# Block attention and MLP on one core: output transposes moved behind the weights' transposes and into their own half of the outputs' bank

## The chip, the cores and the metric

The kernel runs on one core of a Trainium2 chip. The metric is the device time of one execution in microseconds (us). An execution is also profiled: a hardware trace gives start and duration of every instruction on TensorE (PE, with its weight loads as PEld), VectorE (DVE), ScalarE (ACT), GpSimd (POOL) and of the DMA queue that SyncE (SP) issues.

## The reference

Block-sparse attention feeds an MLP. There are 4 batches, 8 heads, 768 positions and 64 values per head; positions come in 24 blocks of 32.

```python
scores = q @ k.T / sqrt(64)
mask = |blk_i - blk_j| <= 1, or blk_i or blk_j is the first or last block,
       or blk_j is one of three sampled blocks of blk_i
attn = softmax(where(mask, scores, -1e9))
x = (attn @ v).transpose(0, 2, 1, 3).reshape(3072, 512)
h = maximum(x @ w_in, 0)                  # w_in 512 x 2048
out = (s * h * h + b) @ w_out             # w_out 2048 x 512
```

Everything is in float32.

## The kernel before

**Slots.** The attention of the first and last query block against all keys is "dense", that of the other 22 query blocks "sparse" (their own three blocks, the two edge blocks, three sampled ones). The work is cut into 52 slots. A sparse slot is one query block of two batches (44 slots, of 22 for each pair of batches), with four units of work; a dense slot is a group of heads of the edge blocks of one batch (8 slots, two units each). Their order is the list `ORD` (line 31): four dense slots, the first pair's sparse slots, four more dense slots woven between the last of these and the first of the second pair's, then the rest.

**A sparse slot.** TensorE makes scores (`scores`, L962) into halves of two PSUM banks. VectorE scales and masks them and takes the row minimum of the negated scores (`maximum`, L980), ScalarE takes the exponential (`exp`, L993). TensorE transposes these weights, eight 128x128 transposes into two banks t (`transposes`, L1023); VectorE evicts the first bank and ScalarE the second (`evacuate`, L1039 and L1041). TensorE multiplies by the values, 64 small matmuls (`av`, L1089; called AV below), into half of the outputs' bank xs; halves alternate from slot to slot. VectorE scales the outputs by one over the row sums into xss (`x_scale`, L1095), TensorE transposes them, two 128x128 transposes (`x_transpose`, L1104; called the pair below), ScalarE copies them to xst (`x_copy`, L1109; four buffers), and SP stores them to DRAM (`spill`, L1116), from where the MLP loads them.

**Dense outputs.** Dense slots evict their weights transposed into dp and the like and wait; 16 sparse slots add 32 matmuls each (`av_dense`, L1079) that sum all eight groups' outputs of two batches in one bank od, a quarter for each slot. When the last of these has run, four dense outputs leave: scale, one transpose within its own quarter of od, copy, two store DMAs (L1120).

**Where the pair stands and where it writes.** Six banks (0 to 5) rotate among scores and t; bank 6 is od and bank 7 is xs. Before the change the pair of slot i-1 stands in slot i between the scores of slot i+2 and the AV of slot i. It writes into the first t bank of slot i, which VectorE has by then evicted; where slot i is dense or missing it takes the next half of xs.

**The order of work.** `Plan` (L109) is a list scheduler that runs when the program is built: each step has an engine, a cost, a priority, dependencies (`deps`, finished first) and places in a queue (`order`, started first), and buffers that it takes (`alloc`) or reads (`use`), with a capacity each (`xst` 4, `xss` 2, `o` 2, `B` 6). TensorE's order in attention is written out by hand (`line`, L1357 to L1365); the other engines take, of what can start first, the step of least priority number. For outputs that is the slot's unit number minus 12, for evictions the unit number minus 8, for exponentials the unit number itself. In the finished program an engine works its queue in order, and semaphores hold each step for the data and buffers that it touches. Decoding of the MLP's weights (L85 to L95) is woven into attention on VectorE, ScalarE and GpSimd. The MLP's first products (L443 to L445) follow attention, its second ones (L485 to L487) wait until all outputs have left the banks they need (`every`, L1373).

Of the kernel before, what the change touches and what calls it, by code (L numbers as in the profile page):

```python
# [212 lines left out]
def kernel(  # L213
# [452 lines left out]
    with ExitStack() as es:  # L666
# [343 lines left out]
        def transposes(n, g):  # L1010
# [4 lines left out]
            if g == 0:  # L1015
                tbank[n] = tp
# [26 lines left out]
        xs_of, xst_of, xss_of, tr_of, tbank = {}, {}, {}, {}, {}  # L1043
# [9 lines left out]
        def goes_on(i):  # L1053
            return i + 1 < len(slots) and slots[i + 1][0] == "s"

        def out_of(i, j):
            if i not in xs_of:
                xs_of[i], tr_of[i] = next_half().rearrange("p (h d) -> p h d", h=4), None
            return xs_of[i][:, j, :]
# [32 lines left out]
        def x_scale(i):  # L1092
            xs = xs_of.pop(i)
            xss = xss_of[i] = xp.tile([P, 4, D], F32, tag="xss", name=f"xss{i}")[:, :xs.shape[1], :]
            nc.vector.tensor_tensor(out=xss, in0=xs, in1=rcs.pop(i).unsqueeze(2).broadcast_to(list(xs.shape)), op=ALU.mult)  # L1095

        def x_transpose(i):
            tr = tr_of[i]
            if tr is None:
                tr = tbank[unit_of[i + 1]][:, :2 * P] if goes_on(i) else next_half()  # L1100
                tr = tr_of[i] = tr.rearrange("p (a q) -> p a q", q=P)
# [4 lines left out]
        def x_copy(i):  # L1106
            tr = tr_of[i]
            xst_of[i] = xp.tile([P, 2, P], F32, tag="xst", name=f"xst{i}", bufs=4)[:, :tr.shape[1], :]
# [73 lines left out]
        spills, tensor, lqs, before, globs = {}, {}, {}, {}, []  # L1182
# [3 lines left out]
        for i, (kind, e, k, r) in enumerate(slots):  # L1186
# [121 lines left out]
            if i and tensor[i - 1][3] and not dense:  # L1308
                tensor[i - 1][3][0].deps.append(evs[0][0])
# [14 lines left out]
            def ends_of(i, u, o_av, dense):  # L1324
                key, rc = (("od", slots[i][1] // 2), ("rd", i)) if dense else (("o", i), ("rc", i))
                to = key if dense else ("B", ("t", unit_of[i + 1], 0)) if goes_on(i) else ("o", ("x", i))
                xc = op("v", 300 if dense else 430, u + T["XA"], lambda i=i: x_scale(i), [o_av, drc[i] if dense else o_rc], alloc=[("xss", i)], use=[key, rc])
                tr = op("p", 270 if dense else 365, u, lambda i=i: x_transpose(i), [xc], cols=256 if dense else 512, use=[("xss", i), to] if dense or goes_on(i) else [("xss", i)], alloc=[] if dense or goes_on(i) else [to])
                ac = op("a", 280 if dense else 390, u + T["XA"], lambda i=i: x_copy(i), [tr], alloc=[("xst", i)], use=[to])
                spills[i] = op("s", 1150 if dense else 600, u + T["SPP"], lambda i=i: spill(i), [ac], use=[("xst", i)], nbytes=66e3 if dense else 131e3)  # L1330
                return tr, ac, xc
# [3 lines left out]
            if k % NBC == 1:  # L1335
# [10 lines left out]
                if not left:  # L1346
                    room = len(slots) - 1 - i
                    for n, m in enumerate(y for y, sl in enumerate(slots) if sl[0] == "d" and sl[1] // 2 == e):
                        late.setdefault(i + 1 + n * min(room, 4) // 4, []).append(ends_of(m, u + 4 + 4 * n, pav, True))
            tensor[i] = s_ops, t_ops, a_ops, trs  # L1350
            before[r] = s_ops, reads
        for i, x in late.items():
            before_it = [tensor[y][3][0] for y in range(i) if tensor[y][3]]
            for n, (tr, _, xc) in enumerate(x):
                xc.deps.append(before_it[-1 if n else -2])
            late[i] = [tr for tr, _, _ in x]
        line = tensor[0][0] + tensor[1][0]  # L1357
# [8 lines left out]
        leave = {id(x) for y in tensor.values() for x in y[3]} | {id(x) for y in late.values() for x in y}  # L1366
# [249 lines left out]
```

## Time and profile before

| | |
|---|---|
| device time, median of 3 runs | 761.25 us (759.11 to 766.74) |
| the profiled execution | 760.56 us |
| its span, first to last instruction | 758.9 us |
| TensorE busy | 732.5 us (97%), 8032 matmuls |
| VectorE, ScalarE, GpSimd busy | 567.8, 472.7, 284.8 us |
| granted TensorE clock, mean | 0.998 |
| share of the chain that ended last: output transposes into t / outputs L1089 / scores L962 / weights' transposes L1023 | 2% / 5% / 5% / 5% |

Attention takes the first 240 us, the MLP the rest. A line such as "PE t L1104" names an engine, the tile that is written and the line of the kernel. In a view of waits, "A <- B" means that engine A was idle until B finished; "issue" means that no semaphore explains the idle time. In a timeline each row is a start, a duration (of a merged run of instructions, first start to last end), engine, line, operation, output<-inputs, and in brackets the idle time of the engine before it.

### The profile page before, as it was taken

The numbers are of one execution on the slowest core, as the hardware profiler recorded it, in microseconds if no ns is written. First come the engines' busy times: TensorE is split into PE (matmuls) and PEld (weight loads), VectorE is DVE, ScalarE is ACT, GpSimd is POOL, SyncE is SP. The second block draws the span as 40 slices with busy tenths as digits, with TensorE's granted clock in tenths as the row PEclk, the third lists the DMA queues.
The fourth block names the chain that finished last, engine by engine and source line by source line (L and its number), as shares of the span: only waits on it lengthen the run. The fifth ranks groups of instructions, "written<-read, shape, count | busy, mean of one in ns | idle before, by whom it ended". The sixth has DMA issues, their size and how long they took to land.

```text
span 758.9 us, 21400 instructions
## 1 busy us (share of the span) xinstructions
PE 732.5 (97%) x8032; PEld 624.0 (82%) x8032; DVE 567.8 (75%) x1436; ACT 472.7 (62%) x1141; POOL 284.8 (38%) x477
## 2 busy tenths in 40 slices
PE   7899999999898999999989999999999999999997
PEld 6576766777677998988878998989989888898896
DVE  3866668988776999987797687797677688666652
ACT  3866668988776887888644443675434566345433
POOL 4977777668641112220022322233222232223221
PEclk9999999999999999999999999999999999999999
DMA  9779778767665346536232230233000022000002
GB/s 266 212 237 282 232 223 240 213 184 217 199 185 155 111 117 217 167 111 161 77 98 83 89 114 28 63 110 86 0 1 1 1 63 84 1 1 0 1 1 83
DMA packets 98743, 89.41 MB, mean 118 GB/s; under 512 B 50352, under 2 KB 79664, under 8 KB 98640
## 3 DMA queue, kind: packets, MB, share of 16 engines
q1 hardware_dynamic: 92544, 71.40, 31.3%
q0 software_dynamic: 6096, 16.65, 7.8%
q8 instruction: 63, 1.03, 0.6%
q14 instruction: 40, 0.33, 0.1%
HBM read 69.15 MB, written 14.68 MB: 110 GB/s over the span
## 4 chain that ended last, share of the span: by engine, by line
PE 84%; DVE 6%; DMA 3%; ACT 3%; issue 2%; SPq 1%; ACTq 0%; DVEq 0%
PE m L622 21%; PE o L486 11%; PE o L487 11%; PE o L485 11%; PE xs L1089 5%; PE s L962 5%; PE t L1023 5%; PE h L443 3%; PE h L445 3%; PE h L444 3%; PE od L1079 2%; PE t L1104 2%; PE t L1021 2%; PE s L941 2%; DVE ptile L980 1%
## 5 line engine op out<-in xcount | busy, mean ns | idle before, releaser
L464 POOL TENSOR_TENSOR hid<-hid,hid 128x384 fp32r<-128x384 f32 x96 | 105.5, 1100 | 297.3 <-ACT hid L640 276.9
L639 ACT ACTIVATE hid<-hid,sb_b,sb_s 128x384 f32<-128x384 f32 x96 | 68.0, 708 | 151.5 <-DVE hid L633 151.5
L993 ACT ACTIVATE ptile<-ptile,nm 128x256 f32<-128x256 f32 (+1 forms) x208 | 107.5, 520 | 45.4 <-DVE nm L980 45.2
L980 DVE CUSTOM_DVE_ANT_1 ptile<-s,mt 128x256 f32<-128x256 f32 x176 | 64.4, 419 | 16.5 <-PE s L962 16.3
L487 PE MATMUL o<-woutr,hid 128*128 128x512 f32 x168 | 66.5, 396 | 0.0
L486 PE MATMUL o<-woutr,hid 128*128 128x512 f32 x168 | 66.3, 395 | 0.0
L485 PE MATMUL o<-woutr,hid 128*128 128x512 f32 x168 | 65.3, 389 | 0.0
L622 PE MATMUL m<-wout,win 128*128 128x384 f32 x264 | 62.2, 339 | 1.0 <-ACT xrest L1509 1.0
L622 PE MATMUL m<-xp,wop 128*128 128x384 f32 x288 | 58.3, 337 | 0.0
L486 PE MATMUL o<-win,hid 128*128 128x512 f32 x144 | 56.8, 395 | 0.0
L633 DVE SCALAR_TENSOR_TENSOR hid<-hid 128x384 f32<-128x384 f32 x96 | 54.3, 565 | 3.3
L622 PE MATMUL m<-xp,win 128*128 128x384 f32 x288 | 55.0, 337 | 1.4 <-DVE xp L606 0.7
L1023 PE MATMUL t<-ident,ptile 128*128 128x128 f32 x352 | 54.5, 297 | 0.5 <-issue 0.5
L622 PEld LDWEIGHTS m<-xp,win 128*128 128x128 f32 x288 | 51.0, 188 | 4.3 <-DVE xp L606 1.2
L640 ACT CAST hid<-hid 128x384 fp32r<-128x384 f32 x96 | 49.4, 514 | 7.8 <-PE o L487 0.4
L622 PEld LDWEIGHTS m<-xp,wop 128*128 128x128 f32 x288 | 51.5, 188 | 2.1
L1023 PEld LDWEIGHTS t<-ident,ptile 128*128 128x128 f32 x352 | 45.7, 208 | 6.7 <-issue 1.1
L907 POOL COPY kk<-kt 128x256 f32 x132 | 50.4, 417 | 0.0
L622 PEld LDWEIGHTS m<-wout,win 128*128 128x128 f32 x264 | 47.5, 188 | 3.3 <-ACT xrest L1509 1.4
L487 PE MATMUL o<-win,hid 128*128 128x512 f32 x126 | 49.8, 395 | 0.0
L485 PE MATMUL o<-win,hid 128*128 128x512 f32 x126 | 49.2, 391 | 0.2
L632 DVE TENSOR_TENSOR hid<-m,xrest 128x384 f32<-128x384 f32 x48 | 26.5, 551 | 30.5 <-issue 25.7
(195 smaller groups left out, 1884.3 us busy)
## 6 DMA issues: line engine op xcount, KB each, us to landing
vB<-in_v_dram SPq DMA_DIRECT2D x76, 128.0 KB, 3.9
raw_o<-in_w_out_dram SPq DMA_DIRECT2D x14, 512.0 KB, 3.6
raw_i<-in_w_in_dram SPq DMA_DIRECT2D x12, 512.0 KB, 3.8
vA<-in_v_dram POOLq DMA_DIRECT2D x46, 128.0 KB, 3.7
xd<-xst SPq DMA_DIRECT2D x44, 128.0 KB, 3.8
vA<-in_v_dram SPq DMA_DIRECT2D x42, 128.0 KB, 4.1
out_dram<-ob SPq DMA_DIRECT2D x20, 256.0 KB, 2.0
sum<-xd SPq DMA_DIRECT2D x12, 384.0 KB, 4.6
```

The lines of the kernel that those rows point to most:

```text
L464: (eng or nc.vector).tensor_tensor(out=htile(5 + i % 3), in0=t, in1=gh.bitcast(F32), op=ALU.subtract)
L485: nc.tensor.matmul(acc, gh[:, tsl], wout(f, 0), start=first, stop=False)
L486: nc.tensor.matmul(acc, gh[:, tsl], wout(f, 1), start=False, stop=False)
L487: nc.tensor.matmul(acc, gl[:, tsl], wout(f, 0), start=False, stop=last)
L622: nc.tensor.matmul(to, w_, x_, start=(c == 0 and k == 0), stop=(c == 1 and k == 2))
L633: vec.scalar_tensor_tensor(out=t, in0=t, scalar=0.0, in1=t, op0=ALU.max, op1=ALU.mult)
L639: nc.scalar.activation(t, t, AF.Identity, bias=sb_b, scale=sb_s)
L640: nc.scalar.copy(gh, t)
L907: nc.gpsimd.tensor_copy(flat(kg[:, a:a + 1]), flat(kts[e][:, bass.ds(j, 1)]))
L980: nc.vector.tensor_tensor_reduce(out=pt, in0=sp, in1=msk, scale=-scale, scalar=FMAX if g == 0 else nm[:, 0:1], op0=ALU.add, op1=ALU.min, a ...
L993: nc.scalar.activation(pt, pt, AF.Exp, bias=nms[n][:, last:last + 1], scale=-1.0, accum_out=dns[i][:, g, j:j + 1])
L1023: nc.tensor.transpose(tp[:, (2 * j + c) * P:(2 * j + c + 1) * P], src[:, c:SW:2], ident)
```

## The change

The pair of slot i-2, not i-1, leaves in slot i, directly behind the transposes of slot i's weights and ahead of the scores of slot i+2 (`leaving`). It writes into the half of xs that held its own outputs before they were scaled; the AV of slot i writes the same half, so it waits until the copy of slot i-2 has read it. The wait of the pair for the eviction of slot i's first t bank is gone, and that bank is no longer held until the copy. Dense outputs still leave one per slot, from the second slot after the last sum instead of the first, with whatever is left behind the last slot; the scaled dense output is put into the xst tile itself, which it thus takes at scaling, and the copy overwrites it. Scaling of a dense output is put behind the transposes of the slot before or behind the copy of the dense output before. Behind the last AV stand the pair of the last slot but one, the left dense outputs, and the last slot's pair. The plan's costs for the transposes are lowered, and the MLP's second products wait for all copies.

```diff
@@ transposes, out_of, x_scale, x_transpose, x_copy
-            if g == 0:
-                tbank[n] = tp
...
-                xs_of[i], tr_of[i] = next_half().rearrange("p (h d) -> p h d", h=4), None
+                o = next_half()
+                xs_of[i], tr_of[i] = o.rearrange("p (h d) -> p h d", h=4), o.rearrange("p (a q) -> p a q", q=P)
...
-            xss = xss_of[i] = xp.tile([P, 4, D], F32, tag="xss", name=f"xss{i}")[:, :xs.shape[1], :]
+            if slots[i][0] == "d":
+                t = xst_of[i] = xp.tile([P, 2, P], F32, tag="xst", name=f"xst{i}", bufs=4)
+                xss = t[:, 1, :].rearrange("p (h d) -> p h d", d=D)
+            else:
+                xss = xp.tile([P, 4, D], F32, tag="xss", name=f"xss{i}")
+            xss_of[i] = xss
...
-            if tr is None:
-                tr = tbank[unit_of[i + 1]][:, :2 * P] if goes_on(i) else next_half()
-                tr = tr_of[i] = tr.rearrange("p (a q) -> p a q", q=P)
...
-            xst_of[i] = xp.tile([P, 2, P], F32, tag="xst", name=f"xst{i}", bufs=4)[:, :tr.shape[1], :]
+            if slots[i][0] == "d":
+                xst_of[i] = xst_of[i][:, :1, :]
+            else:
+                xst_of[i] = xp.tile([P, 2, P], F32, tag="xst", name=f"xst{i}", bufs=4)
@@ plan
-            if i and tensor[i - 1][3] and not dense:
-                tensor[i - 1][3][0].deps.append(evs[0][0])
...
-                to = key if dense else ("B", ("t", unit_of[i + 1], 0)) if goes_on(i) else ("o", ("x", i))
-                xc = op("v", 300 if dense else 430, u + T["XA"], lambda i=i: x_scale(i), [o_av, drc[i] if dense else o_rc], alloc=[("xss", i)], use=[key, rc])
-                tr = op("p", 270 if dense else 365, u, lambda i=i: x_transpose(i), [xc], cols=256 if dense else 512, use=[("xss", i), to] if dense or goes_on(i) else [("xss", i)], alloc=[] if dense or goes_on(i) else [to])
-                ac = op("a", 280 if dense else 390, u + T["XA"], lambda i=i: x_copy(i), [tr], alloc=[("xst", i)], use=[to])
+                xss = ("xst" if dense else "xss", i)
+                xc = op("v", 300 if dense else 430, u + T["XA"], lambda i=i: x_scale(i), [o_av, drc[i] if dense else o_rc], alloc=[xss], use=[key, rc])
+                tr = op("p", 260 if dense else 265, u, lambda i=i: x_transpose(i), [xc], cols=256 if dense else 512, use=[xss, key])
+                ac = op("a", 280 if dense else 390, u + T["XA"], lambda i=i: x_copy(i), [tr], alloc=[] if dense else [("xst", i)], use=[key, *([xss] if dense else [])])
...
+                copied.append(ac)
...
-                    room = len(slots) - 1 - i
...
-                        late.setdefault(i + 1 + n * min(room, 4) // 4, []).append(ends_of(m, u + 4 + 4 * n, pav, True))
+                        late.setdefault(min(i + 2 + n, len(slots)), []).append(ends_of(m, u + 4 + 4 * n, pav, True))
...
-            before_it = [tensor[y][3][0] for y in range(i) if tensor[y][3]]
-            for n, (tr, _, xc) in enumerate(x):
-                xc.deps.append(before_it[-1 if n else -2])
+            for n, (_, _, xc) in enumerate(x):
+                xc.deps.append(tensor[i - 1][1][-1] if n == 0 else x[n - 1][1])
...
+        def leaving(i):
+
+            return [*(tensor[i - 2][3] if i - 2 in tensor else []), *late.get(i, [])]
+
...
-            ahead = tensor[i + 2][0] if i + 2 in tensor else []
-            leaves = [*(tensor[i - 1][3] if i else []), *late.get(i, [])]
-            line += leaves + ahead if slots[i][0] == "d" else ahead + leaves
+            line += leaving(i)
+            line += tensor[i + 2][0] if i + 2 in tensor else []
             line += tensor[i][2]
+        line += leaving(len(slots)) + leaving(len(slots) + 1)
...
-        every = [ac, o_av, *ends]
+        every = [o_av, *copied, *ends]
```

## Rows read from the trace of the kernel before

**Rows 1.** Busy time of the engines in stretches of the span (us from its start): TensorE with its count of matmuls, its weight loads, VectorE, ScalarE, GpSimd, then the granted clock, the DMA engines' share and GB/s.

```profile
60.00:100.00 40.00, 36.54 (x1023) 27.16 (x1019) 25.93 (x106) 26.06 (x90) 28.47 (x62) 1.00 0.85 260
...
120.00:157.00 37.00, 35.99 (x770) 26.27 (x772) 34.56 (x126) 32.70 (x103) 25.80 (x53) 1.00 0.74 211
157.00:229.00 72.00, 68.71 (x2001) 51.86 (x1998) 59.22 (x226) 55.92 (x183) 44.43 (x98) 1.00 0.67 198
229.00:239.00 10.00, 7.02 (x166) 5.53 (x162) 6.85 (x17) 6.67 (x20) 0.54 (x1) 1.00 0.59 145
...
280.00:360.00 80.00, 80.00 (x401) 72.23 (x400) 68.51 (x130) 66.82 (x118) 14.74 (x16) 1.00 0.54 163
```

**Rows 2.** Waits of TensorE between 100 and 245 us: who waited for whom, us in total, times, the longest.

```profile
PE t L1104 <- DVE pt L1039: 3.4, 5, 1.2
PE od L1104 <- ACT xst L1109: 1.8, 1, 1.8
...
PE od L1104 <- DVE xss L1095: 0.6, 1, 0.6
PE t L1023 <- issue: 0.5, 1, 0.5
```

**Rows 3.** The same view between 60 and 100 us.

```profile
PE xs L1089 <- issue: 2.3, 3, 1.2
PE s L962 <- issue: 1.0, 1, 1.0
```

**Rows 4.** The chain of work that ended last, in order of time, through sparse slots in the middle of attention: start, us, what.

```profile
160.87 1.15 PE t L1023 x8
162.02 1.02 PE s L962 x32
163.04 0.37 PE t L1104 x2
163.41 1.03 PE xs L1089 x64
...
187.78 1.08 PE od L1079 x32
```

**Rows 5.** Timeline around three dense slots: weights' transposes without a pair behind them (28.13), with a pair (144.00), scores followed by AV (148.64), VectorE's eviction ahead of that AV, and a pair that waited for an eviction (154.74).

```profile
28.13 1.97 PE L1021 MATMUL t<-ident,ptile 128*128 128x128 f32 x16
30.03 1.09 PE L962 MATMUL s<-kk,qr_0s 64*32 64x256 f32 x32
...
144.00 1.97 PE L1021 MATMUL t<-ident,ptile 128*128 128x128 f32 x16
145.80 0.38 PE L1104 MATMUL xs<-ident,xss 128*128 128x128 f32 x2
146.11 1.09 PE L962 MATMUL s<-kk,qr_3s 64*32 64x256 f32 x32
...
148.64 1.09 PE L962 MATMUL s<-kk,qr_4s 64*32 64x256 f32 x32
149.73 0.32 PE L1089 MATMUL xs<-vA,pt 128*32 128x64 f32 x8
...
154.74 0.44 PE L1104 MATMUL t<-ident,xss 128*128 128x128 f32 x2 [0.65 <-DVE pt L1039]
...
149.00 0.67 DVE L1039 COPY pt<-t 128x512 f32<-128x512 f32 x1
```

**Rows 6.** The instructions of line 1104 that write into t: count, duration ns least/median/most, first and last start.

```profile
L1104 PE MATMUL t<-ident,xss x78: 272/300/332, 38.3 to 234.9; 128*128 128x128 f32 x78
```

**Rows 7.** The tail: timeline of TensorE, VectorE and ScalarE at the last dense outputs, and one piece of the chain of work that ended last.

```profile
237.64 0.33 PE L1104 MATMUL od<-ident,xss 128*128 128x128 f32 x1 [1.75 <-ACT xst L1109]
...
235.31 0.29 DVE L1095 TENSOR_TENSOR xss<-od,rc 128x128 f32<-128x128 f32 x1 [0.18 <-PE od L1104]
...
237.32 0.27 ACT L1109 COPY xst<-od 128x128 f32<-128x128 f32 x1 [0.98 <-DMA xd<-xst]
...
232.32 4.92 DMA xd<-xst
```

**Rows 8.** Timeline of two sparse slots: weights' transposes and the pair on TensorE, scaling on VectorE, the copy on ScalarE.

```profile
160.80 1.22 PE L1023 MATMUL t<-ident,ptile 128*128 128x128 f32 x8
...
162.97 0.44 PE L1104 MATMUL t<-ident,xss 128*128 128x128 f32 x2
...
161.53 0.41 DVE L1095 TENSOR_TENSOR xss<-xs,rc 128x256 f32<-128x256 f32 x1
...
164.06 0.35 ACT L1109 COPY xst<-t 128x256 f32<-128x256 f32 x1
164.37 1.23 PE L1023 MATMUL t<-ident,ptile 128*128 128x128 f32 x8
...
164.85 0.40 DVE L1095 TENSOR_TENSOR xss<-xs,rc 128x256 f32<-128x256 f32 x1
```

**Rows 9.** Timeline of the sparse slot with the latest copy: pair and copy.

```profile
73.11 0.44 PE L1104 MATMUL t<-ident,xss 128*128 128x128 f32 x2
...
74.63 0.35 ACT L1109 COPY xst<-t 128x256 f32<-128x256 f32 x1
```

**Rows 10.** The DMA issues of line 1120, the stores of dense outputs: duration ns on SP's queue, least/median/most.

```profile
L1120 SPq DMA_DIRECT2D xd<-xst x16: 360/460/1808, 127.1 to 239.2; - x16
```

More of the change, by code (lines that the diff above doesn't have):

```diff
@@ L1041, in evacuate @@
                 nc.scalar.copy(o, src)
-        xs_of, xst_of, xss_of, tr_of, tbank = {}, {}, {}, {}, {}
+        xs_of, xst_of, xss_of, tr_of = {}, {}, {}, {}
         turn = [0]
@@ L1051, in next_half @@
             return box["o"][:, turn[0] % 2 * 2 * P:][:, :2 * P]
-        def goes_on(i):
-            return i + 1 < len(slots) and slots[i + 1][0] == "s"
         def out_of(i, j):
             if i not in xs_of:
-                xs_of[i], tr_of[i] = next_half().rearrange("p (h d) -> p h d", h=4), None
+                o = next_half()
+                xs_of[i], tr_of[i] = o.rearrange("p (h d) -> p h d", h=4), o.rearrange("p (a q) -> p a q", q=P)
             return xs_of[i][:, j, :]
@@ L1181 @@
         lastk = {}
-        spills, tensor, lqs, before, globs = {}, {}, {}, {}, []
+        spills, tensor, lqs, before, globs, copied = {}, {}, {}, {}, [], []
         costs = {"s": (515, 580, 258), "d": (725, 450, 780)}
@@ L1359 @@
             line += tensor[i][1]
-            ahead = tensor[i + 2][0] if i + 2 in tensor else []
-            leaves = [*(tensor[i - 1][3] if i else []), *late.get(i, [])]
-            line += leaves + ahead if slots[i][0] == "d" else ahead + leaves
+            line += leaving(i)
+            line += tensor[i + 2][0] if i + 2 in tensor else []
             line += tensor[i][2]
+        line += leaving(len(slots)) + leaving(len(slots) + 1)
         for prev, o in zip(line, line[1:]):
             o.order.append(prev)
-        leave = {id(x) for y in tensor.values() for x in y[3]} | {id(x) for y in late.values() for x in y}
-        leave = [o for o in line if id(o) in leave]
-        for prev, o in zip(leave, leave[1:]):
-            o.deps[0].order.append(prev.deps[0])
+        for leave in ([x for i in tensor for x in tensor[i][3]], [x for i in sorted(late) for x in late[i]]):
+            for prev, o in zip(leave, leave[1:]):
+                o.deps[0].order.append(prev.deps[0])
         last = tensor[len(slots) - 1]
-        assert all(i < len(slots) for i in late)
         o_t, o_av, ends = last[1][-1], last[2][-1], [y for x in evs.values() for y in x]
-        every = [ac, o_av, *ends]
+        every = [o_av, *copied, *ends]
         op("s", 450, N - 60, lambda: nc.sync.dma_start(out=sb_s, in_=s_in.rearrange("(a o) -> a o", o=1).broadcast_to([P, 1])))
```

## The prediction, on record before the changed kernel ran

> **What bounds the kernel now.** I read the waits of TensorE first, then its busy time by stretches, then the chain of work through the clean middle of attention, and only then the places where the output transposes stand. In [rows 1] the reader is to see that between 280 and 360 us TensorE is busy 80.00 of 80: whatever attention gives up moves the end by as much, as long as the matmuls that follow have their weights and inputs. Attention, before that, leaves TensorE idle 3.5 us of the 40 between 60 and 100, 1.0 of 37 between 120 and 157, 3.3 of 72 between 157 and 229 and 3.0 of 10 at its end. [rows 2] say for whom it stops after 100 us: mostly for the output transposes (L1104), 3.4 us behind VectorE's eviction of the weights' transposes and 2.4 us at the dense outputs. Between 60 and 100 the stops have no semaphore behind them, 3.3 of those 3.5 us [rows 3]. Nothing in the change touches them, so I let them swallow what is saved around them. [rows 4], the chain in clean sparse slots, give the unit of the sum: transposes of weights 1.16, scores 1.02, output transposes 0.37, outputs (AV) 1.03, together 3.58 us, plus 1.08 in the 16 slots that also carry dense outputs' sums.
>
> **The change, part by part.** *Place of the pair.* Between scores and AV the two output transposes cost 0.37. Directly behind transposes they stand already in the dense slots: transposes begin at 144.00, the pair at 145.80, the scores at 146.11, where without a pair transposes to scores took 1.90 (28.13 to 30.03) [rows 5]. The pair thus costs 1.80 + 0.31 - 1.90 = 0.21 there. Scores followed at once by AV took 1.09 (148.64 to 149.73), against 1.02 before a pair; that AV waited for an eviction that ended at 149.00 + 0.67 = 149.67 [rows 5], so the extra lies between nothing and 0.07. The saving is 0.37 - 0.21 less 0 to 0.07: 0.09 to 0.16 a slot; I take the middle, 0.12. There are 39 such pairs (78 transposes into t, [rows 6]). Ten lie among the stops without a cause, two beside VectorE's busiest stretch (34.56 of 37 us, [rows 1]); 27 x 0.12 = **3.2 us**. The ends are 27 x 0.09 = 2.4 and 39 x 0.16 = 6.2.
>
> *The wait for the eviction.* AV needs the same eviction, so the wait stays; but the pair no longer stands behind it. The pair at 154.74 started when the eviction released it [rows 5], and AV could come only 0.37 after [rows 4]. Of the five waits of [rows 2] three stand ahead of the tail; they give 2 x 0.37, and 0.37 - 0.12 for the one that is among the 27: **1.0 us**. It is nothing where VectorE, late there, is late for the next step instead.
>
> *The tail.* In the ten us around the last two slots' transposes and AVs TensorE works 7.02 and is idle 3.0 [rows 1]. With outputs two slots late, these slots' AVs follow without the stands; the work only moves: one sparse pair and three dense outputs go behind the last AV, among MLP matmuls. What AV still waits for its eviction and what the pair saves there about cancel, so 3.0 us come free. Against it stand the store buffers. There are four; of the copy whose store left at 232.32 the buffer was free only 4.92 us later, and TensorE stood 1.8 us for it [rows 2, 7]. Eight outputs leave in this stretch, and a dense one now takes its buffer when it is scaled on VectorE, one engine earlier, with the MLP's VectorE steps queued behind that scaling. I charge 1.5 us (0 to 3.6, none or two such stands). Net **1.5 us** (-0.6 to 3.0). The MLP's second products wait for the last copy; the first products cover that, and without them it would cost what the late outputs need.
>
> *New waits.* An output's transposes now write the half of the outputs' bank that AV two slots on will fill, so AV waits for ScalarE's copy. Its price is not in the trace; I bound it by the typical copy. The pair would start 1.16 - 0.10 = 1.06 after the slot's transposes begin (1.90 and 1.80 in [rows 5] differ by that 0.10), end 0.38 later at 1.44, and AV would come at 1.06 + 0.31 + 1.02 + 0.07 = 2.46. The copy starts 0.65 after its pair's end (163.41 to 164.06) and takes 0.35 [rows 8]: 2.44, in time by 0.02. In [rows 9] it starts 1.08 late and would end at 2.87. The lower end is nothing; the upper is the slower rival. Most copies in the trace lie near the first, so I charge 0.03 x 27 = **0.8 us**. Behind a waiting AV stands all of TensorE, but ScalarE's exponentials have room: no wait of L1023 on ScalarE is in [rows 2]. The release of the t bank one copy earlier I cost at nothing: no scores wait for a copy in [rows 2]. Nor do I charge the store that moves one slot later with its two DMA issues for a dense output (2 x 0.46 us of SP's queue, [rows 10]): the same stores stood in that queue before, and the value loads behind them land for AVs that wait for no DMA in [rows 2]; without that cover a late copy would hold those loads on SP. POOL's queue gets nothing new. Weights' decoding moves with the plan; its cover is VectorE's idle time outside 120 to 157.
>
> Sum: 3.2 + 1.0 + 1.5 - 0.8 = 4.9 us off the profiled execution's 760.56 us (span 758.9 and 1.7 around it): 755.7. The median of the runs shown, 761.25, is 0.7 above it, so I say **756 us**.
>
> **The rivals.** *The bank goes over as a whole: no change.* In the tail the dense outputs share one bank, each in its own quarter. The transpose at 237.64 waited for ScalarE's copy at 237.32 of another quarter, and VectorE's scaling at 235.31 for a transpose into another quarter [rows 7]. If the two halves of the outputs' bank are handed over likewise, the pair of two slots back waits for the scaling of the last slot, which it does not read. That scaling ended 0.88 after the slot's transposes began (164.37; 164.85 + 0.40) and 1.14 after (160.80; 161.53 + 0.41) [rows 8], the pair being due at 1.06. In the 28 slots without dense sums a hold of 0.1 to 0.2 each, 2.8 to 5.6 us, would eat what the place of the pair saves: 759 to 762 us. [...] For the rival: the scaling ends within a tenth of the due time. Against: that is a tie, not a delay, and 16 slots have 1.08 us more. *TensorE is not what sets the pace*: stops without a semaphore and VectorE take the rest; also 759 to 761. Together 0.27.
>
> *All of it comes through:* 6.2 + 1.0 + 3.0 = 10.2 us, 751 us; for it speaks how clean the slots of [rows 4] are. 0.26.
>
> *Slower: AV behind a late copy.* ScalarE takes its queue in order. If the eviction and exponentials stand ahead of the copy as in [rows 9], AV comes 2.87 - 2.46 = 0.41 late, and 44 x (0.41 - 0.09) = 14 us are lost: 775 us. It decides from a copy that starts 0.65 + 0.02 + 0.12 = 0.8 us or more after its pair in most slots. Against it: ScalarE is busy 55.92 of 72 us there [rows 1], and the plan ranks the copy ahead of evictions and exponentials. 0.08.
>
> **How the numbers follow.** The forecast has 0.39, with 753.6 to 759 as its own range. What a measurement can tell is about 1%, 7.6 us: under 753.6 is faster, over 768.9 slower. Faster has the second-last case, 0.26; slower the last, 0.08; the rest, 0.66, lies within 1%. The range takes in the full gain and the no-change cases: 750.5 to 761.5.
>
> **What would show it.** Sparse slots of about 3.46 us instead of 3.58, with the pair 0.2 wide behind transposes; no wait of L1104 on the eviction, but some of L1089 on it; the last AV some 5 us earlier. Wrong would be: L1089 waiting for ScalarE's copy (L1109) slot after slot, L1104 waiting for the scaling (L1095), or TensorE standing among the first MLP matmuls for dense outputs.

## The result, and the profile after

The changed kernel takes **767.28 us** (median of 22 runs, 762.42 to 771.37), the one before 762.48 (22 runs, 758.54 to 767.36): a ratio of 1.0056, 95% interval 1.004 to 1.0073. I had said 756.0, with a range of 750.5 to 761.5. The profiled execution after took 764.83 us, span 762.8, so 3.9 us more of span than before. A profile shows one execution, and the 22 of one kernel differ by up to 9 us here: the profiled ones of e2, e8, e13 and e14 below (769.5, 767.06, 763.94 and 775.79 us) lie 3 to 4 us above the medians of their kernels. Line numbers move: weights' transposes are L1021 (dense L1019), dense sums L1076, AV L1086, scaling L1097, output transposes L1103, the copy L1111, evictions L1037 (VectorE) and L1039 (ScalarE); scores stay L962 (dense L941).

Busy time of the engines in the stretches of [rows 1]; after each time the count, last the granted clock, the DMA share and GB/s:

```profile
60.00:100.00 40.00, 35.06 (x978) 26.33 (x974) 24.75 (x104) 25.47 (x89) 26.55 (x59) 1.00 0.84 242
120.00:157.00 37.00, 32.74 (x683) 25.29 (x673) 31.54 (x116) 30.41 (x95) 23.30 (x50) 0.95 0.71 204
157.00:229.00 72.00, 65.60 (x1937) 49.82 (x1940) 57.91 (x220) 54.74 (x179) 48.61 (x103) 1.00 0.69 202
229.00:239.00 10.00, 8.85 (x281) 7.50 (x270) 7.21 (x28) 8.10 (x26) 1.08 (x2) 1.00 0.19 59
280.00:360.00 80.00, 80.00 (x403) 72.54 (x402) 68.19 (x126) 67.14 (x119) 15.81 (x17) 1.00 0.53 159
```

The MLP stretch is as full as before: what attention loses or gains moves the end. From the first of the MLP's second products to the end it takes 511.9 to 512.3 us in all sixteen traces. TensorE is now busy for less time in each of the first three attention stretches, and one of them, the woven one, no longer has its full clock.

Waits of TensorE from 20 to 262 us (us, times, longest), the view of [rows 2] over all of attention:

```profile
PE xs L1086 <- issue: 4.3, 7, 1.1
PE xs L1086 <- ACT pt L1039: 3.8, 2, 2.2
PE od L1076 <- issue: 3.4, 3, 1.4
PE s L962 <- issue: 2.3, 3, 1.2
...
PE xs L1086 <- ACT xst L1111: 1.3, 2, 1.2
PE t L1021 <- issue: 1.3, 1, 1.3
...
PE xs L1103 <- DVE xss L1097: 0.8, 2, 0.6
```

The waits of the output transposes for VectorE's eviction, 3.4 us in [rows 2], are gone but for one of 0.4 us. In their place the four rows without a semaphore ("issue") come to 11.3 us. The same rows of before, over the same stretch, came to 5.5:

```profile
PE xs L1089 <- issue: 2.7, 4, 1.2
...
PE od L1079 <- issue: 1.3, 1, 1.3
...
PE s L962 <- issue: 1.0, 1, 1.0
...
PE t L1023 <- issue: 0.5, 1, 0.5
```

The second of these rows lies in the stretch of [rows 2], among the lines that are not printed there. Evictions now hold AV, 3.8 us in two waits.

Where nothing interferes the slot is shorter, as meant (timeline of TensorE):

```profile
108.45 1.22 PE L1021 MATMUL t<-ident,ptile 128*128 128x128 f32 x8
109.51 0.38 PE L1103 MATMUL xs<-ident,xss 128*128 128x128 f32 x2
109.82 1.09 PE L962 MATMUL s<-kk,qr_2s 64*32 64x256 f32 x32
110.84 0.32 PE L1086 MATMUL xs<-vA,pt 128*32 128x64 f32 x8
...
111.88 1.22 PE L1021 MATMUL t<-ident,ptile 128*128 128x128 f32 x8
```

1.06 to the pair, 0.31 to the scores, 1.02 to AV, 1.04 to the next slot: 3.43 us, against the 3.58 of [rows 4]. So the question is where some 40 times 0.16 us went.

To answer it I add up TensorE's blocks (transposes, pair, scores, sums, AV) from their weight loads, from the AV of slot 4 to the AV of slot 42 (here and below slots with a number are the 44 sparse ones, counted from 0), and hold each against its own undisturbed duration (the lower quartile in that kernel). "Inside" is what blocks take longer within themselves: stops without a semaphore, a slower clock, in both kernels one wait of 1.4 us for VectorE in the middle of scores and, some 2 us of it among the dense slots of before, short pauses within scores that no view names. "Between" is waiting from one block to the next; a wait that comes back in nearly every slot hides in "undisturbed" instead. How the lower quartile is taken moves up to 1.5 us from one of these three columns to another, in e7 more. The last column is the tail, from the AV of slot 42 to the MLP's second products.

```
us                       all   undisturbed  inside  between   tail
before                  179.9     164.8      11.6     3.4     14.8
after                   186.3     159.4      19.4     7.5     13.2
before, run again       180.4     164.8      10.5     5.1     14.9
after, run again        186.6     159.4      19.7     7.4     13.2
```

Undisturbed time fell by 5.4 us and the tail by 1.6; inside grew by 7.8 and between by 4.1. With 1.0 us gained ahead of slot 4, that is the 3.9 us of the span. In the second pair of traces the AV of slot 4 came 0.6 us later than before, not 1.0 earlier, so that gain may be chance; the other columns moved the same way, and the span grew by 5.1 us. The stops without a semaphore came again too, 5.8 and 12.3 us in the view of waits.

**Inside: stops at every 256th instruction.** One stop in TensorE's timeline, in the middle of an AV:

```profile
77.31 0.75 PE L1086 MATMUL xs<-vA,pt 128*32 128x64 f32 x35
79.13 0.64 PE L1086 MATMUL xs<-vA,pt 128*32 128x64 f32 x29 [1.08 <-issue]
```

I count TensorE's instructions, weight loads, matmuls and semaphore instructions together. In the two kernels 18 steps within a block take over 0.7 us (from 30 to 235 us); 16 of them lead to the 194th or 195th instruction of a piece of 256, and the other two wait for a semaphore. The DMA section of the profile's page has the queue that belongs to it:

```profile
q8 instruction: 63, 1.03, 0.6%
```

63 packets, each of 16,384 bytes in the trace. Before the stop above a packet began at 76.70 and took 1.05; TensorE went on 1.38 us after its end. TensorE's queue has 16,282 instructions in this trace, counted as above, and 16,240 in that of the kernel before: 258 to a packet in both. From these counts, and from the places of the stops, I take a packet for one piece of 256 instructions. What they cost is not small: the four rows of after come to 11.3 us.

**Between: the woven stretch.** VectorE, ScalarE and TensorE of after, where dense slots stand among sparse ones:

```profile
136.50 0.29 DVE L1097 TENSOR_TENSOR xst<-od,rc 128x128 f32<-128x128 f32 x1 [0.57 <-ACT ptile L993]
...
137.75 0.67 DVE L1037 COPY pt<-t 128x512 f32<-128x512 f32 x1
...
136.91 0.61 ACT L993 ACTIVATE ptile<-ptile,nm 128x384 f32<-128x384 f32 x1
...
137.51 0.57 ACT L1039 COPY pt<-t 128x512 f32<-128x512 f32 x1
...
133.72 1.23 PE L1021 MATMUL t<-ident,ptile 128*128 128x128 f32 x8
...
138.53 0.32 PE L1086 MATMUL xs<-vA,pt 128*32 128x64 f32 x8 [2.23 <-ACT pt L1039]
```

The transposes began at 133.72, but VectorE scales a dense output (after a wait of 0.57), takes two sparse row minima and a reciprocal before it evicts at 137.75; ScalarE runs its dense exponentials first and evicts at 137.51. In the kernel before, the same eviction came right behind the dense row minima, with transposes that began at 133.18:

```profile
134.85 0.69 DVE L1039 COPY pt<-t 128x512 f32<-128x512 f32 x1
```

The view names ScalarE's copy for TensorE's stop of 2.23 us; that copy ended at 138.08 and VectorE's at 138.42, right ahead of the AV, so VectorE's is the likelier cause. The stop is followed by a stretch at a lower granted clock (windows as above):

```profile
138.00:140.00 2.00, 1.47 (x64) 1.41 (x64) 1.93 (x6) 1.08 (x5) 1.04 (x2) 0.75 0.56 158
140.00:142.00 2.00, 2.00 (x16) 1.92 (x10) 1.73 (x7) 0.60 (x2) 0.00 (x0) 0.50 0.40 97
142.00:144.00 2.00, 2.00 (x22) 1.49 (x24) 1.08 (x2) 1.39 (x3) 0.00 (x0) 0.90 0.59 161
```

The AV there took 0.41 and the sixteen dense transposes 1.11 longer than undisturbed: 1.5 us of "inside" that the wait brought with it.

**The tail** of after (ScalarE, then TensorE):

```profile
235.49 1.32 ACT L414 CAST xp<-xraw 128x384 fp32r<-128x384 f32 x3
236.71 0.57 ACT L1039 COPY pt<-t 128x512 f32<-128x512 f32 x1
237.19 0.36 ACT L1111 COPY xst<-xs 128x256 f32<-128x256 f32 x1
...
237.61 0.32 PE L1086 MATMUL xs<-vA,pt 128*32 128x64 f32 x8 [1.15 <-ACT xst L1111]
```

Here AV does wait for the copy of two slots back, which stands behind casts of MLP inputs. It is the one long wait of that kind.

### The profile page after: what moved, and what is told of

Its sections match the earlier page's. It is cut to its first block, busy times and chain, and to the rows that moved or that the text cites. A ratio compares the mean times of both kernels' runs of the same rounds, so it can differ in the third digit from the quotient of the medians.

```text
span 762.8 us, 21487 instructions
## 1 busy us (share of the span) xinstructions
PE 729.2 (96%) x8032; PEld 624.3 (82%) x8032; DVE 565.8 (74%) x1436; ACT 472.5 (62%) x1141; POOL 286.3 (38%) x477
## 4 chain that ended last, share of the span: by engine, by line
PE 79%; DVE 9%; ACT 4%; issue 4%; DMA 2%; POOL 1%; SPq 1%; POOLq 0%; ACTq 0%; DVEq 0%
PE m L622 20%; PE o L486 10%; PE o L487 10%; PE o L485 10%; PE s L962 5%; PE xs L1086 5%; PE t L1021 5%; PE h L443 3%; PE h L445 3%; PE h L444 3%; DVE ptile L980 2%; PE od L1076 2%; PE xs L1103 1%; DVE xp L606 1%; PE t L1019 1%
## 5 line engine op out<-in xcount | busy, mean ns | idle before, releaser
L1086 PEld LDWEIGHTS xs<-vA,pt 128*32 128x32 f32 x1696 | 35.4, 110 | 27.2 <-ACT xst L1111 12.9
L486 PE MATMUL o<-win,hid 128*128 128x512 f32 x144 | 56.8, 394 | 0.0
L1021 PE MATMUL t<-ident,ptile 128*128 128x128 f32 x352 | 54.1, 296 | 1.3 <-issue 1.3
L1086 PE MATMUL xs<-vA,pt 128*32 128x64 f32 x1696 | 46.9, 223 | 8.2 <-ACT pt L1039 3.8
L1021 PEld LDWEIGHTS t<-ident,ptile 128*128 128x128 f32 x352 | 45.6, 208 | 7.3 <-issue 3.1
L487 PE MATMUL o<-win,hid 128*128 128x512 f32 x126 | 49.8, 395 | 0.0
```

The costliest lines, as they stand in the source:

```text
L486: nc.tensor.matmul(acc, gh[:, tsl], wout(f, 1), start=False, stop=False)
L487: nc.tensor.matmul(acc, gl[:, tsl], wout(f, 0), start=False, stop=last)
L1021: nc.tensor.transpose(tp[:, (2 * j + c) * P:(2 * j + c + 1) * P], src[:, c:SW:2], ident)
L1086: nc.tensor.matmul(xs[quads[pair]], pt[:, c, quads[pair]], vt[:, a, col:col + D], start=(j == 0 and c == 0), stop=(c == 1), tile_position= ...
```

## The experiments

Ratios are to the kernel before on the same chip, with 95% intervals; where there was a single run no interval is given. The account of above for all of them, the two repeated runs aside (e3, e4, e5 and e10 carry fewer bytes):

```
us                              all   undisturbed  inside  between   tail
e1  dense outputs earlier      186.0     159.3      20.9     5.8     13.2
e2  evictions first            190.2     159.6      26.5     4.1     13.4
e3  before, quarter values     170.3     165.0       3.1     2.2     16.6
e4  after, quarter values      175.7     159.3       8.6     7.9     13.2
e5  e2 with quarter values     174.9     159.3      10.2     5.3     13.5
e6  two output banks           187.4     160.9      20.3     6.2     13.2
e7  pair one slot back         195.7     187.9       4.0     3.6     14.5
e8  before, evictions first    184.7     164.8      15.3     4.7     16.4
e9  e6 and e2                  188.0     160.0      20.2     7.9     13.2
e10 e9 with quarter values     174.6     159.9       7.7     7.0     13.3
e13 before with the new tail   183.6     162.9      14.3     6.2     13.2
e14 pair done twice            193.0     167.4      16.0     9.6     13.9
```

In e7 most of the waits shown below, 19.8 us, come in every slot and so stand in its undisturbed column.

**Do the stops come from the load on the DMA queues?** From slot 10 of the 52 on, the value loads carry a quarter of each row in e3 (before) and e4 (after), and in e5 and e10 below; the other three quarters of those values are left out. The edit for the sampled blocks is shown; the window's loads have the same.

```diff
-            on.dma_start(out=vt[a::4], in_=src[bass.ds(j, 1)].rearrange("o e a d -> (o e) a d"))
+            x = src[bass.ds(j, 1)].rearrange("o e a d -> (o e) a d")
+            on.dma_start(out=vt[a::4] if i < 10 else vt[a::4, 0, :DM // 4], in_=x if i < 10 else x[:, 0, :DM // 4])
```

> The kernel before, with three quarters of the bytes of the window's and sampled blocks' value loads left out from slot 10 on (same number of DMAs, same program order). Theory 'instruction supply': TensorE's stops without a semaphore all lie at the same place of every 256 instructions, and are long while the DMA engines are loaded; with fewer bytes their sum (10.9 us of steps between 20 and 245 us) falls below 6 us and the kernel is 3 to 5 us faster: ratio 0.994 to 0.996. Rival 'the stops have nothing to do with DMA load': they stay, ratio 0.999 to 1.001.

> The changed kernel with the same three quarters of the value bytes left out. Theory 'instruction supply': 0.16 us that a slot saves was swallowed by longer stops (17.7 us of steps); with these short, the changed kernel gains 7 to 9 us on itself, and stands at or below the kernel before with the same bytes left out: ratio to before 0.993 to 0.997. Rival: the loss has other causes, the changed kernel gains no more than the kernel before does, and stays 4 to 5 us behind it.

e3: 752.21 us, 0.986 (0.9833 to 0.9887). e4: 754.71 us, 0.9879 (0.9852 to 0.9906). Fewer bytes take 10.8 us off the kernel before, where I had expected 3 to 5, and 12.6 off the changed one, where I had expected 7 to 9. From 50 to 112 us the DMA engines' share falls from 0.83 to 0.50 in e3. With these bytes gone the two kernels differ by 0.0019 and their intervals overlap. In the waits of e3 the stops without a semaphore have shrunk from 5.5 us to one row:

```profile
PE xs L1090 <- issue: 0.6, 1, 0.6
```

In e4 they are 4.3 us (1.7, 1.1, 0.8 and 0.7). So the stops hang on the load, but at the same load the kernel with shorter slots has more of them, and it does not get ahead without the load: against e3 it has 5.7 us less undisturbed time, 5.5 more inside and 5.7 more between. The packets of the instruction queue bear on why. Mean times from one 256th instruction to the start of the next packet, its duration, and from its end to the next 256th instruction (pieces with exactly one packet, 10 to 14 of each; in us):

```
              from 50 to 112 us               from 158 to 220 us
before    2.17 + 1.16 + 1.52 = 4.86       1.40 + 1.11 + 2.09 = 4.60
after     2.44 + 1.11 + 1.42 = 4.97       2.14 + 1.03 + 1.64 = 4.82
e3        1.45 + 1.16 + 1.94 = 4.55       0.89 + 1.14 + 2.37 = 4.40
e4        1.77 + 1.34 + 1.46 = 4.57       1.56 + 1.11 + 1.85 = 4.51
e7        1.53 + 1.22 + 2.44 = 5.19       1.18 + 1.13 + 2.65 = 4.97
```

The third term never falls under about 1.2 us in before and after (1.26 and 1.21 at the least): in these two no piece is used sooner after it lands. In the first stretch of after its twelve values lie between 1.21 and 1.55, near that floor, so there probably nearly every piece is waited for; before, eleven of twelve lie under 1.75. TensorE with shorter slots reaches the end of a piece sooner, and the next packet then starts later after it, 2.44 instead of 2.17 and 2.14 instead of 1.40. 256 instructions take no less time than before (4.97 against 4.86, 4.82 against 4.60), though the slots' own work is shorter. Between e3 and e4 the sum stands still as well, 4.55 and 4.57. (The change also puts 42 more semaphore instructions into TensorE's queue, 218 instead of 176; that is a sixth of one piece, too little to make the difference.)

**The woven stretch.** e1 lets the first half's dense outputs leave one slot earlier; e2 ranks the sparse slots' evictions ahead of row minima, exponentials and the scaling of outputs; e8 makes the edit of e2 in the kernel before; e5 is e2 with a quarter of the values' bytes.

```diff
@@ e1, in the kernel after
-                        late.setdefault(min(i + 2 + n, len(slots)), []).append(ends_of(m, u + 4 + 4 * n, pav, True))
+                        late.setdefault(min(i + (2 if e else 1) + n, len(slots)), []).append(ends_of(m, u + 4 + 4 * n, pav, True))
@@ e2, in the kernel after (the priority of an eviction)
-                    o_ev = op(on, {"a": 690 if dense else 590, "v": 745 if dense else 690}[on], n + T["EV"],
+                    o_ev = op(on, {"a": 690 if dense else 590, "v": 745 if dense else 690}[on], n + (T["EV"] if dense else -30.0),
```

> The changed kernel, with the first four dense outputs leaving one slot earlier (from the first slot after the last sum, as before the change); all else as changed. Theory 'dense outputs': between the AV at 120.5 and the one at 155.2 the changed kernel needs 34.7 us where the kernel before needed 30.9, because the dense outputs' scaling and copy stand in VectorE's and ScalarE's queues ahead of evictions that AV waits for. Moved back, the stretch needs 31 to 32 us and the kernel is 3 to 4 us faster than the changed one: ratio to before 1.000 to 1.002. Rival 'queue order at large' (the evictions slip behind row minima whatever the dense outputs do): the stretch stays near 34.7 and the ratio at 1.005.

> The changed kernel, with the plan's priority of sparse evictions raised ahead of row minima (unit number minus 30 instead of minus 8). Theory 'eviction behind row minima': in the dense-woven stretch AV at 129.2 and 138.5 waits 1.5 and 2.2 us for an eviction that VectorE makes only after row minima and a dense scaling; with the eviction first these waits go below 0.5 us each and the kernel is about 3 to 4 us faster than the changed one, ratio to before about 1.001. Rival 'engines full': VectorE and ScalarE are the limit there, the minima come later instead and the weights' transposes wait; ratio stays at 1.005.

> The changed kernel with both edits of earlier runs: sparse evictions planned ahead of row minima, and three quarters of the value bytes left out from slot 10 on. With the instruction stops mostly gone and the waits in the dense-woven stretch gone, what the change saves in TensorE's work (44 slots at 0.16 us, and 2 us of the tail) should show: theory 'swallowed savings' expects 750 to 751 us, 1 to 2 us ahead of the kernel before with the same bytes left out (752.2). Rival 'the change itself costs': it stays at 754 to 755 as without the eviction edit.

> The kernel before, with sparse evictions planned ahead of row minima. In the kernel before the pair and AV stood 2.4 us for evictions ahead of the tail. If those waits go and nothing swallows it: ratio 0.997. Theory 'instruction supply': shorter slots only lengthen the stops at every 256th instruction, ratio 0.999 to 1.001.

e1: 765.44 us, 1.0029 (1.0007 to 1.005). AV's waits for evictions in the woven stretch fall from 4.9 to 2.5 us, which fits a ratio 0.0027 lower, though the intervals overlap. From the AV of slot 19 to that of slot 23 it needs 33.2 us, against 34.7 in the changed kernel, 30.9 in the one before and the 31 to 32 that I had expected. e2: 766.2 us, 1.004 (1.0021 to 1.0059). There these waits are gone, and in the profiled execution the stops took the room; in its waits of TensorE, beside 3.0 us on two other lines, stand

```profile
PE xs L1086 <- issue: 9.2, 10, 1.9
PE s L962 <- issue: 5.0, 4, 2.7
```

17.2 us instead of 11.3, in an execution 3.3 us above the median; a median one may have less. e5: 753.15 us, 0.9866 (0.9834 to 0.9897), where I had looked for 750 to 751: not told apart from e3, and not faster. e8: 763.23 us, 1.0001 (0.998 to 1.0023). Its edit did not take away the waits that it was meant for: the pair still waits 3.5 us for evictions in five waits, against 3.4 before. So e8 tests neither case.

**Is the outputs' bank handed over as a whole?** e6 gives the two halves a bank each, taken from the rotation of scores and t. e7 keeps the pair in its own half but lets the pair of slot i-1 leave, between scores and AV, as before the change; AV of slot i then writes the other half while that pair is being copied. e9 is e6 with e2's priority, e10 is e9 with a quarter of the values' bytes.

```diff
@@ e6
-    NBANK = 6
+    NBANK = 5
-                box["o"] = bank(NBANK + 1, "xs")
+                box["o"] = [bank(NBANK + 1 + n, f"xs{n}") for n in range(2)]
-            return box["o"][:, turn[0] % 2 * 2 * P:][:, :2 * P]
+            return box["o"][turn[0] % 2][:, :2 * P]
@@ e7
-            return [*(tensor[i - 2][3] if i - 2 in tensor else []), *late.get(i, [])]
+            return [*(tensor[i - 1][3] if i - 1 in tensor else []), *late.get(i, [])]
-            line += leaving(i)
-            line += tensor[i + 2][0] if i + 2 in tensor else []
+            ahead = tensor[i + 2][0] if i + 2 in tensor else []
+            line += leaving(i) + ahead if slots[i][0] == "d" else ahead + leaving(i)
```

> The changed kernel with the two halves of the outputs in two banks of their own; scores and weights' transposes rotate over five banks instead of six. Theory 'a bank goes over as a whole': the pair's waits for the scaling of the slot before (L1103 on L1097, 2.1 us of gaps between 160 and 233 us) vanish, to below 0.3 us; what five banks cost elsewhere is open, so the total may be anything from 1 us faster to 5 us slower than the changed kernel. Rival 'the pair waits for its own data or for VectorE's eviction': the gaps stay at about 2 us.

> The changed kernel with the pair of the last slot, not the last but one, between scores and AV (where it stood before the change), still writing into its own half of the outputs' bank. Theory 'a bank goes over as a whole': AV, which writes the other half, waits in every sparse slot for ScalarE's copy, 0.5 us or more each (copy 0.35 and two hand-overs): about 20 us slower than the changed kernel, 780 to 795 us. Rival 'only the columns count': AV waits for nothing new, 763 to 769 us.

> The changed kernel with the outputs' halves in two banks and sparse evictions planned ahead of row minima. Theory 'instruction supply': both edits take waits away (T to X 2.1 us, S to AV in the dense-woven stretch 3 to 5 us), but the stops at every 256th instruction grow by most of it: ratio 0.998 to 1.002, stops of 12 us or more. Rival 'the waits were the whole loss': ratio 0.993 to 0.995, faster than both kernels.

> The same with three quarters of the value bytes left out from slot 10 on. Theory 'instruction supply': with the stops small, the saved work shows; 749 to 751 us against 752.2 of the kernel before with the same bytes left out (0.9825 to 0.985 of the kernel before). Rival 'the saving of 0.16 a slot does not reach the end for another reason': 753 us or more, as without the two banks.

e7: 780.68 us, one run. TensorE's waits:

```profile
PE xs L1086 <- ACT xst L1111: 19.8, 39, 0.5
...
PE xs L1086 <- issue: 0.4, 1, 0.4
```

39 AVs wait half a microsecond each for a copy out of columns that they do not write: the bank goes over as a whole. (These waits stand at semaphores that the program sets, and both halves belong to one tile xs as well as to one bank. No run separates tile from bank.) And the stops without a semaphore have all but vanished, 11.3 to 0.4 us, in a kernel with the same transfers whose slots are half a microsecond longer; its third term in the table above is 2.44 and 2.65. The load per time falls with the longer slots, from 50 to 112 us from 0.82 to 0.74 of the DMA engines; e14 below has 0.76 there and keeps its stops, so that alone does not do it.

e6: 766.42 us, 1.0029 (1.0001 to 1.0056). After the change the waits between transposes and pair come to 2.13 us from the AV of slot 24 to that of slot 42; with two banks they are 0.09, and no wait of L1103 for scaling is left. The lower ratio fits those 2 us, but its interval meets that of the changed kernel, and undisturbed time is 1.5 us more, perhaps for the bank that scores and t have less. e9: 765.59 us, 1.0044 (1.0019 to 1.0069), where I had expected 0.998 to 1.002; its stops, 15.7 us, are the 12 or more that I had expected. e10: 754.36 us, 0.9894 (0.9862 to 0.9925); I had expected it under 751. Removing both waits, even with the load taken off, does not bring out the saving: in e10 AV waits 3.8 us for ScalarE's copy, which e3 does not, scores and dense transposes 4.1 us for row minima, and the stops are 5.1 us.

**How far do two runs of one kernel differ?**

> The kernel before once more, for the spread of its stops from run to run: theory 'instruction supply' expects them again at the same instruction of 256, with a sum near the 6.5 us beyond normal steps of the first profile (5 to 9).

> The changed kernel once more: stops at the same instruction of 256, with a sum near its first 12.1 us (10 to 15), above that of the kernel before. If the two sums overlap, the difference of the first pair of profiles was chance and the stops don't explain the loss. The waits of AV in the dense-woven stretch (4.9 us) and of the pair (2.1 us) should come again within 0.5 us.

761.05 and 766.47 us. The accounts repeat to 1.7 us in a column (table in the first section), so differences of 2 us in it carry little and those of 5 do. AV's waits in the woven stretch came again with 4.6 us and the pair's from slot 24 to slot 42 with 2.1, as expected.

**The tail alone, and longer slots.** e13 is the kernel before in which only the last four sparse slots' pairs and the second four dense outputs leave as in the change (its core below). e14 is the changed kernel with each sparse pair done twice.

```diff
@@ e13, in the kernel before
+        TAIL = len(slots) - 4
...
-            leaves = [*(tensor[i - 1][3] if i else []), *late.get(i, [])]
+            leaves = [*(tensor[i - 1][3] if i and i - 1 < TAIL else []), *(tensor[i - 2][3] if i - 2 >= TAIL else []), *late.get(i, [])]
...
-                        late.setdefault(i + 1 + n * min(room, 4) // 4, []).append(ends_of(m, u + 4 + 4 * n, pav, True))
+                        late.setdefault(min(i + 2 + n, len(slots)) if e else i + 1 + n * min(room, 4) // 4, []).append(ends_of(m, u + 4 + 4 * n, pav, True))
@@ e14, in the kernel after
-            for pr in range(tr.shape[1]):
+            for pr in list(range(tr.shape[1])) * (2 if slots[i][0] == "s" else 1):
```

> The kernel before up to its last four sparse slots; these four and the last four dense outputs leave as in the changed kernel (pair two slots later, into its own half; scaled dense outputs in the store's tile). In both profiles of the changed kernel the tail gained about 2 us, where the DMA engines are little loaded. Theory 'where instructions come in time, saved work counts': ratio to before 0.997 (0.995 to 0.999). Rival 'the tail's gain is given back in the first MLP products': 0.999 to 1.002.

> The changed kernel with the two transposes of each sparse slot's outputs done twice, same data to the same place (4 instead of 2 matmuls, about 0.22 us of TensorE's work more in 44 slots, 9.7 us in all; no other engine, DMA or wait changes). Theory 'instruction supply sets the pace in the loaded stretches': the stops at every 256th instruction shrink from 11 to 12 us to about 6 to 8, and the kernel is only 3 to 7 us slower than the changed one: ratio to before 1.009 to 1.015. Rival 'TensorE's work sets the pace and the stops come on top': all 9.7 us arrive, ratio 1.017 to 1.019, stops as before.

e13: 760.25 us, **0.996** (0.9927 to 0.9992): the only version without missing bytes that is faster than the kernel before, and faster than the changed one. The upper end of its interval is close to 1. Its profiled execution has the longest stop of the study, again at a 256th instruction:

```profile
195.82 1.56 PE L1024 MATMUL t<-ident,ptile 128*128 128x128 f32 x6 [4.97 <-issue]
```

The packet ahead of it began at 193.15, 6.3 us after the last 256th instruction (186.85). The tail is 13.2 us long, as in the changed kernel.

e14: 772.8 us, 1.0114 (1.0069 to 1.0159). Undisturbed time grew by 8.0 us over the changed kernel, inside fell by 3.4, between rose by 2.1, and the ratio grew by 0.0058, 4.4 us. The time is the one that I had expected, 1.009 to 1.015, but the stops are not: in the view of waits they come to 11.3 us, as in the changed kernel, and not to 6 to 8. Two thirds of the fall of "inside" are one stop (2.15 us, at 65.87) that lies between two blocks here. That part of the added work hides in the stops, as in e7, is therefore not shown by e14.

## Why the prediction was wrong

*The place of the pair* (3.2 us). The saving per slot was right and at the upper end, 3.43 us instead of 3.58 where I said 3.46; scores followed at once by AV cost nothing extra (1.02). Undisturbed time fell by 5.4 us, within my 2.4 to 6.2; it holds a stand of 1.15 us that belongs to the tail, and without that the fall is 6.5, just over. One reading was off: between 60 and 100 us the trace has eight pairs, not ten, which is worth 0.2 us.

*The step that failed* is the sentence on the stops that [rows 3] show: "Nothing in the change touches them, so I let them swallow what is saved around them", which I applied to ten slots and let the other 27 count in full. The change touches them by making the slots shorter. Where I saw 1.0 us of 37 and 3.3 of 72 idle in [rows 1], I read room for the saving; but stops of the same kind stood there already, 1.8 of the 3.3 us (1.3 in the row of L1079 above and 0.5 in [rows 2]), and the 256 instructions of a piece took no less time there when their work was shorter. The column "inside" grew by 7.8 us, 4.6 up to the AV of slot 19 and 3.4 from that of slot 24 on. In between it hardly moved: 1.5 us of lower clock came and the short pauses of before went. In the view of waits the stops grew from 5.5 to 11.3 us. Two pairs of traces show this at full load and e3 against e4 at the lower one. The stops all but go in the kernel before with fewer bytes (e3), and in the changed one with half a microsecond more in each slot (e7). With 0.2 us more they stay (e14). The rival "TensorE is not what sets the pace" had this mechanism, but as a zero sum; that waiting would grow by more than the saving was in none of my cases.

*The wait for the eviction* (1.0 us gained). Between slots 4 and 19 and from 24 on the pair's waits for evictions, 1.0 and 1.3 us, did go. In the woven stretch the term has the other sign: AV waits 4.9 us there, where the pair and AV together had waited about 1. I had let "It is nothing where VectorE, late there, is late for the next step instead" stand as the worst case. The plan put evictions behind row minima, exponentials and a dense scaling, and behind the longer of the two stops that this made, 2.23 us, the lower clock cost another 1.5. e1 halves these waits, e2 removes them; neither gets more than about 2 us for it.

*The tail* (1.5 us gained) came out in size, in part by luck: from the AV of slot 41 to the MLP's second products 19.8 us became 18.0, 1.8 less. The 1.5 us that I charged there came as one stand of 1.15 us, ahead of the AV of slot 42, for a copy that was late behind casts, not as the wait for a store buffer that I had named. With the tail alone e13 is 0.4% faster (0.1 to 0.7), more than these 1.8 us, 0.2%, explain.

*New waits* (0.8 us). AV behind ScalarE's copy cost 1.3 us in two waits, nearly all in the tail; elsewhere the copy was in time, and the slower rival that rested on it is refuted, 775 us did not come about that way. What I had as a rival, *the bank goes over as a whole*, holds: e7 shows it at 0.5 us a slot, and in the changed kernel the pair waits 2.1 us for a scaling of the other half that ends just too late. My price for it, 2.8 to 5.6 us, was a little high; it is one loss among three, not the whole case. With a bank and a tile for each half the pair's waits are 0.09 us (e6); whether it is the bank or the tile that is handed over, no run shows.

So the sum that I made as -3.2 - 1.0 - 1.5 + 0.8 is, by the account: 5.4 of place, 1.6 of tail and 1.0 ahead of slot 4 gained; 7.8 inside blocks and 4.1 of waits lost, of these about 4 in the woven stretch; 3.9 us slower. In the second pair of traces 5.4 of place and 1.7 of tail were gained, and 9.2 inside, 2.3 of waits and 0.6 ahead of slot 4 lost; 5.0 us slower.

Three things stay open. With the load reduced and both waits removed (e10) the changed kernel still does not beat e3; 7.7 us inside against 3.1 and other waits of 7.0 against 2.2 are where the time is, but no run separates them. How much longer a slot must be before the stops shrink lies between e14 and e7, and e7 is a single run. And that a packet starts late because other transfers stand ahead of it is inferred from e3 and e4; no record shows when it was asked for.

## What to carry to other kernels

Idle time that no semaphore explains is a bound like any other: count the engine's instructions between such stops, and if they lie at a fixed number, work made shorter in front of them may not be saved until the instructions come sooner. Fewer bytes on the queues at that time did it here (e3: 5.5 us of such stops became 0.6); fewer instructions were not tried. When a step moves in a hand-written order, look at where the planner then puts the steps that it waits for; two late evictions and the clock behind them cost, by the account, about what forty shorter slots gave, though moving them forward (e1, e2) gave back no more than about 2 us. The part of a change that frees a stretch with real waits (here the tail) can be worth taking alone (e13).

## What the runs showed of the hardware

In the two kernels instruction pieces of 16,384 bytes went into use no sooner than about 1.2 us after they had landed (1.26 and 1.21 at the least). Their packets began 0.9 (e3) to 2.4 us (the changed kernel) after the previous 256th instruction on average, later at the higher load; one began 6.3 us after it, and TensorE stopped for 4.97 us (e13).

TensorE's granted clock fell to 0.50 during attention in all but two of the sixteen traces (e4 and e5), for some microseconds each time (3.4 in each of the two kernels): behind a stop of 2.22 us at 8.56 in the kernel before, of 2.23 at 136.30 in the changed one, of 4.97 at 190.85 in e13. Behind the 1.75 us in [rows 7] it did not fall; behind 1.65 us at 104.44 in e2 it did. Where it falls, a stop costs more than its own length: 2.23 us and 1.5 us of slower work behind it in the changed kernel.
